# Gated linear attention and a rational MLP on one core: k's turn in the second attention bank, with a new table of steps

## The chip, the cores and the metric

One core of a Trainium2 chip runs the whole program in one launch. The metric is device time in microseconds (us). The kernel before takes 522.44 us (median of 3 runs, 521.91 to 522.75).

## The reference

Four inputs q, k, v, alpha of shape (4 batches, 8 heads, 768 tokens, 48) in float32 give a linear attention with a decay per channel; its output, seen as 3072 tokens by 384, goes through an MLP whose activation is a rational function:

```python
for t in range(S):                       # attention, per batch and head
    state = alpha[t][:, None] * state + outer(k[t], v[t])
    y[t] = q[t] @ state
h = x @ w_in                             # x: (3072, 384), w_in: (384, 2048)
P = a[0] + a[1]*h + a[2]*h*h + a[3]*h*h*h
Q = 1.0 + abs(b[0])*abs(h) + abs(b[1])*h*h
out = (P / (Q + 1e-06)) @ w_out          # w_out: (2048, 384)
```

## The kernel before

**Steps and tables.** The kernel is cut into 2737 steps. Each is a small function that issues a few instructions on one engine (SP for DMAs, PE, ACT, DVE, POOL). They are added with a name, an engine, for some a second engine (`alt`), and the steps that they must follow (`after`, lines 978 to 1185). The order in which they are issued is not worked out at run time: it is read from `ORDER` (line 77), a packed list of step numbers in which the top bit chooses the second engine. Each engine's queue holds its steps in that order. A step's costs and due times in `add` are not used when the table is read.

**Attention.** The 3072 tokens are 24 groups of 128, six for each batch. For group g: `suf` and `pre` (lines 475 and 487) are scans on DVE over alpha, which read a floor value, for g of 4 and over, from column 500 of PSUM bank 5 (`floor_q`, line 361); `k` and `q` (POOL or DVE) multiply the inputs with them. On PE come four small steps: `kt` (line 549) turns k with 4 transposes; `s` (512) makes the scores; `vk` (577) multiplies turned k with v for the state; `am` (590) multiplies the masked scores and the state with v. Between them stand `ke` (553, ACT copies the turned k out of PSUM), `qc`, `se` (523, 532, copies of the scores, ACT or DVE), `sm` (543, mask, POOL), `km`, `kv` (606, 612, DVE adds up the state), `dc`, `mc` (560, ACT or POOL puts the state beside v), and after `am` the output is copied by `xh` (ACT, 626) and `xl` (DVE, 642). All of this works in two PSUM banks, `SCB` = 4 and `SCB + 1` = 5: scores in columns 0 to 255 of both, state products in columns 256 to 447 of both, turned k in columns 0 to 447 of bank 4, the output of `am` in columns 0 to 511 of bank 4.

**MLP.** 96 units u of 128 hidden columns by 512 tokens, or the like. `in` computes h on PE in bank u mod 3; `ah`, `t1`, `rcp` (ACT), `q1` (ACT or POOL), `qm` (POOL), `t2`, `t3`, `p`, `t`, `g` (DVE) give the rational function; `oh`, `ol` (PE) multiply with w_out, after `gh` (ACT) and `gl` (POOL or DVE) have cut g into two parts. Units 0 to 9 are "plain" (lines 677 and 690), the others "wide" (700 and 714), 9 matmuls in `in` and 9 in `oh` and `ol`. `in` of unit u waits for `g` of unit u - 3, whose bank it takes.

**Weights.** 16 blocks come in as 64-bit words (`w`, SP) and are joined to float32 in four steps: `abs` (ACT 285), `low` (DVE 293), `sign` (297 on ACT, 299 on DVE), `join` (DVE 313). Then `hi` and `lo` split them for the wide units.

**The end.** 36 `gu` steps on ACT (line 863) check alpha; `vd_sum` (DVE), `vd_mm` (PE), `vd_ok` (DVE) make one number of them, which all engines read at line 1192, and a branch takes a general program if alpha is out of bounds.

The wait for the copies of the last group's output is in these lines: `was` names the steps of group g - 1 that touch the two banks.

Of the kernel before, what the change touches and what calls it, by code (L numbers as in the profile page):

```python
# [19 lines left out]
AF = mybir.ActivationFunctionType  # L20
# [4 lines left out]
class Plan:  # L25
# [49 lines left out]


ORDER = [
    'c-jq?gO(*a5CGGi?sSs1ZQHhO+qS)XcV>35wr$(CZQHi--Zxa8Qx!=~R!X6YsiG-Sq*yr>Lm3rCMOS0hI5l3)SBunQ6;-WN',
    'vD6y1L`_i3l~+?#WHnVSP)pS+bzMzT6IC}{sFnq~V-HNN(yBCSePFFh7g(WsVlV8CeXws(KkSbKaRg3NGt_D|00-e&eNL}a',
    'u~l3ZN5u<FSNqiY;K4Wq=cu`Ai`uOAs||sn7{K9}UX@m5)l4;8%~J7Ixj=4}R|N+hQrp!wbx`F~dDJEa3Mo2mRKqX~!*Pe2',  # L80
    'r?#q-DznO>f-p2F1V>_-zy+--0uQUnI0Y|itq!Q2>a<F%PN@s(naZ!qtKETJfu!nEaI!#F#YAK&2F0Y<A)|0K8WK99jwwg6',
    'C@$?$wbfpAMV(PsRXi%JE~&=qvAV3zspG1$dY~?<6Dlc<!Erb~Xd-%wL`T&mOhzdvIb~BxR9#h1)lrdY0*=M0I4$Ugnt_*f',
    '6q=54C_Y`$DJi)sqME9rs+h`5S?H>siL<boN<cSNLaMK_tKzDvT7-*(Qc)sGO;ITt&Bi&n1k+G9%1Sw@wQ8&8;sRWTX(=6@',
    'S7+5VwG;=ahw72a9<mVU;e5<N8*x+6ZDmz@%0(HdiK?b<sr%}+%1wEwASI?GREP@Ga?D8Aba|>knW!igqwD&HUV(SiTa}lJ',
    'P;q*v+Nm}wAJwILRDznTfO@VvsVb_v3Q}FvAoW8%RXtU2wGu1QDjcXPQdKHRrRa%zrCzGL>V;Z^>v1hs4yi)xuo~s30#u(G',
    'P-$uyvH=^>8}&hzq3TqF?y1$d8Mg%0q{dW>now8OS#?wGRWH>?^;Lt_5Y?K>QX6VYZK)acQ~d)S)Hb}S+fxVXNxi5y4OQi+',
    '9c{$}*fDSpo6{}*UVT)3sUIE0?y5(iHf_f`)Q5K9SM^hUQwn~oFY2HAt^geTQemnEwWI)bBn_RYGX<;RYB+sXpVThwPk+@P',
    'g<zly4WNP4l?b}gPTY-qa32n$5H&0iL?JYS_Tye`McrvI9m2yngct<I(m0w&J!n1!Qz(s49%6xoC=eYYK?0RfB??4_xDXTK',
    'Kn#cmQ6Y@R(*%kS6KN7nrf`a&BY0bf2Ex?>8cKKcQ9OntX%Q`^DKwQvQ38k!@gNZlqvLo2&*MovgVQJ>B!-K42dC3QT0$3a',
    '21Tf)w4OH5MmmLO@ieATDItT(s8T>ml?;+YCfFP@lV;Ht8ckzp6K$mfbdWCLY??#MXgRH*m2{Cts=NB0zKq-G5{*)aXceud',  # L90
    'BXpFu(+)aJ$7m-Vr(HCc)=*MN0vVwYq=ht)0aC#gyo#6U3SFm6fva?lPS8oZhWGF~?xq`f6W7u@dPI+DFYTjSco%QueSC;F',
    '=oH<gbdVa-LuNQlS>P$%qCNDCUQ%wz55*uK<b?uIK;?l{fgGwR<bs?~7z#oWI74S?Kb@od`hosM&*=r-rmXOa?oc)ut;Pgi',
    '(;NCtk@*k(r6_!!?$SSs$_3R0Dh@TF0=%UMm>nJ=@H=`>_bCZKprnjk67Eqnen>G{@nh6XoC7{kbdJFlp%PSvLV*e@ImhCh',
    'Dpw#jGbiH|oRVK-35dgn<8mr~icjz(eWGXh5}#u{{!HKK3kh3}&oA&5Cg9ZkgR*iqF2-p%EobMPoQrdC4JZdypoFRl?Vt`c',
    'hw{)AigP+H!KJt~=jM{^*mERK$cZ>TXW)!nQB?{wg9fSvROcG}gc5Tm&dgc(E#~38T!zbXKF-hOxIDkX0$d7eaZN4*wYd%#',
    '<U-tnTXJE3haa${Dix@}^`Iix<yKsYD|2ahkM;N$c7%uek!}OEp%yfT)?A+(a64|O%0e4%%Z&m(xfl25KKvVta8dq<pRfuy',
    '<i6aGt8z8&4DGoCH{!<p8NcEe{DD8QhN`J*1)6Y2?$2GI6A$2TIFLJY7w*c{pe0m?y3iVWK`ZDBO}QBda|lo7DLjJ1IGhLZ',
    'U=HP}{0INyG#<j=@gI8K5F&UakK*RsjhFCJ?#|PBC=cVAJcE^ftVi=0t`B2*E05y_&<J{PfVc57Ue2?4Hm~57+yRC{A84U^',
    'Lre8UgGRlb+e2Fz3{7AN4Cf$T#ls*RR`VJj&;LhBv);j0&*8Z|kB{+jKEZ2w9UDELPw{SU6_~*5c_Lru8$5|4U?B8|LC_OA',
    '!33BHBViQufUz*p4}hH`A_Y4gS?}UKyqBZuC|Yzhy^t620zS!$`6hRRuFxI!@qRwQFZik6z#I9Qj;?R>Ek46%c{rTr1o|!q',  # L100
    '!9705lVKBY=7StVpXUpFk?-(*P8fWMUvf+xTgTFgbmHJGe3;|txH_JWuP^as{>i^Mi9W(d`4ztz@s=NOKL|hwJmg3Gn&0tz',
    '{=@$`omM6oM!<9ZLSNy>{DiOaHI8XwnWy}h!F=G4jOG)6=2T{|*M>}N^M&J@q&k^?#{K+Um=AMc63l~8V6y_o!z`EzaZG%Z',
    '+I;1-CXF#h%m6>gCou6$LNf-!AcY<cUuhitr0=v5(uJls8B9i#$^7QzI;BppGwR$Xl}@dna~@;OH~!8)*qKBouSsk&n<OTU',
    'PHM`SEGB<wKI2VU6Uk&Xb<GqgXbPERro2h3Gw4h@x|s%1O=OeYlrxn~WmCXZ2+gCjnf|`8DPpEWQB%y+Gbv0;lf&dR*-b7}',
    '(KIks%u8L>v@^v`ebe4_Ff-tl&aAWOYNom=Y5JSlupAb_W>^NBU<)jP1rYGNU_I=FrLYhd!(Lbgjm>e$rW=NqFda=7GZV7v',
    'CZ?3BVLF-8rk3ey^65sVsmZQ8n{KA2Sq;rh-rxedw9cV(>Rft&8E6KX{JOarY=)TbriE!~TAA9Wj_F}~nqH>2$*m*INHfZ`',
    'Hf_vIGt0C!eavVx)U1JFCSdl%7&F$)Hgn8MI04&W2W*AmCdiC4!KR>ot+&H&*Z_OrG@OECa1xHfDl^`Mm<gt@S#93vwNOa+',
    'Gofa<FRa&?bx>3n(fi;r%r_IwBr`X3o>^cfn-ONM*<dcgMzhc?GEd+loPlDxxSnE4>O-(DbiLVR7MmsJ2t0)#AL{SHZnMYi',
    'HRs?04Dq+&Jlusl5N5*7G;_wBHPg*hv(L;hOU-_B&K!WUx|A*#yxEk{Wr8c{TkuvNge~R@Y&Cbya<j~wH!I9abI=?zm&^fk',
    '7!I2Y=AzkVwwrglysoG#>C5Jdxe7<jJ#*hYFh|Y9&|12-eq@fB<K~2^qATln=Dpcru9|D+gZUKt**rGa;JT@!>ju};Ps~oU',  # L110
    '%bYYyKu(#{=7zatZkwCtA)JNF5Y0S;2k;1<!w2|izL>A3s;;4{>8IwId2Xufn!3Io>QTO#@8*SxAu;8Sd9Po>5A#7^hX(qm',
    '$sif!rFm_%7#Zec%SZSGH{m{fhVO6#TIyFOjs*Mn&`^i_`0@%wqL>#D4P%%uKw+(dSsLkI#!3Ql(nLqWukZ{0fS|+1y0!Ka',
    'Nis>?uy~SC-k7&0mi#e)O>_MZew)aWSz72e!BM2CZl?d4f>KBdOCnL2SdvIK$u3DH%omXmKf-%_2L?y`cAD@fM3qWXSzbeN',
    'DIr<HvdSCCAw|QANlB?9ZFMrKD$yjmB$pJDQgTWz$t|U%w3Ly?(nPvQ5B*Vp((QFRsUfK(jdYbfl2@8ZwXmjAR^CDfT~n${',
    'EomvOq`B0VI+9O1>5jUWt}ErFn{?JKq_wn>w$dZ4r*xNIQcuSE{8B*5O9dG!!=$1#kZ!t*?ipNP8cHK+C%tuV=_7#Mbyppb',
    '_A*@hN<Zl@9VAGCWt@zcs2Jg6pvCAI86)9u_yO~!kM1a)q_ZrLQGTKfkbx2+Bjg(}{)N;M6BA)lOpK{835H6TgiC~c))Qom',
    'PlFTvAQ>zh1o4aRtEb4Mu*ot~M#(~1B#R|2Cc{{m8xvr1OpQ~epPnX5Wtqgr=`urR%0}5Nn`DVBmm#uE2561_^*}u+c!jK#',
    'I5<mY%NE%xqh*X7ltXe@j)onRVS22rl1p+~w#yDVA^{y2hwIg{MuzC2da#}&b7h{am36XHcF9P;TOP|E*(>qzxSWtHa#F6z',
    'b$KFJ<(aIPVEt96#5|Y~v*9>j0MlW1OfQ8n1s24dm>=_EF3g9gBm<t7GjdkW$rt%5`{b$Ikc@a!Zb^_HqvPXqc_H6)h`ud%',
    '<hy*65&DPxl$Y{KUdw(tAa`Ygzb9jZ@5?U<)#3WLgz0hmjl7ji_)h-U+FI+wBiZr6=jDQ2lm`;eK9u;@*+24ECi}=Xiv1_)',  # L120
    'u^KA-ULy1;{YXB_C;1?w^+-KYN3|1lG#lN<un8>K%$O)Vu}yC?*w2#DPVx!ucb&v0wLkPEUEG$iS+NvWz{;2dOJfy8t1a1N',
    'Hn~k<i(pDy!;bfv?G&HMX0h39b~{^VwJ~k1@EkUk&1rMl!kF8#O>Ils(&1%n7OZJ&*;2NwEoW=n$-15`ih1l*U*1-*v27e1',
    '*XFf#!t2^JHmz-GTiNM;hM(rA>M6Q9R>Z1U9@9!$tY|CQUbeTbZ|CaydQNa_+ctcaZfD!r_O^qarYqY9wxMlg8{6r6hMuYC',
    '>5jIOO=t7j{I(btu!U_?oaH;)g0_$CXPelWKE#f&p>~#DpnvKrwu_x&r`lh-sI6+N*`~Gx_P5pTLR}n7VprSOhS>pjpdD!k',
    '*}-;*U8KukGc00<+PS_QHnYub3)|iHur;tTw!um`-_P^YY;&xSi+uxZg2ikr3=fa6-RyMR(+;ys?J_&u&a$KIY&+VHv19Ex',
    'J0m<`XWBV-g<Wpv+Ie=oo$V*sm3Ea~te5H~I>@fJ^X&?~Qm?UV?KZpJ2HOR8p*?OV+DUe@t%d9Cdb>ui4L)HP*~NB)y<wNw',
    'n|7z&VOQ&2cDLPQ_u6Ipq+R1rhcDOr>_)rEuG9PN0ejHCw43cId)A(_OZ_c-$DXn0?IF8U-?cUIg1u<h>)*OIUb27mZ9B)`',
    'vvu&kt&3aiR{P2xwr}hPy;1+Nm+h7C*Y>S_XOGyU_LzNdAJ~Vs9)7SN?IZix{<eSYF8$YDwNLC*yIF724Y3gxvR$zycER0x',
    'kKUrU>#e#iezM>`+b{O3jqIYhs4lv@X0O|S;mV=Y?wL*Ep4+4@nR{W|<6eD2@6fGrfp38wupMsGG2A!%-9~fd{@*0m31hmB',
    'D9*ahxKAf{DO^ey%Vl*xY&Q4PrgDGvKfPbac5z&47uUse*<H?vT+TV~PU-{tpgyEe=^QS%OXK3Z1TK#|tWWD>`nXQ((zzqS',  # L130
    'd0jpi$rW?OT|$@0C3Z*k8C}wqj!5q^xJ)jy%jojE0!|T7Jy+kAa%Ei^SI(7p?Og}gz%_D>T|-yURd5wu7T3{LasymtSJ*Xi',
    'O<gnB+!b=2Tvyk^E%5{0AXmh-blqGPH`onxog=!q?rx#);R3Fw>*a>Hp{}T_>RP$hZn&%Fs=JY{maE}<yFRXttLtjJAUDd5',
    'c4OT*7wkgZEH~TDbz|HdH!ot5Z{ym!c5b!n>-xF=ZjBr7Cb)@igq!3hy9I8co8soXMQ*WM;?}yUZoLb0;ck!H>z2B+F4V1a',
    '5pJ2=;5NEVZnN9srn&v@kX!EdxdRag-Bx$lZFA?`c{kn7a5LQscfnnD_uPHA-R*D}-6glut#UivE_cLTaYx-%cg#I-k0Kts',
    '<L-nz>8`o!?xB0)p1No5z5C!kx!vxRyWzm2f9_7Zo9?4~;l8?W?xlO>wErCO#eH|TBG~_MKOK4T*8g(GpK-7MhwA-p7t_b`',
    'cU)}$+r=Fj&);=_+#8q5zjdkoJNMVc@$r2EpU_A0k$oDUZe${#)@Se;eR`kCNAXd8VxPq4_IZ3>|Id|h$|v>7d>LQX=lA)1',
    'W}n4p^>uwTAKl0B1$`l3-k0;)d?jDN7xooKR`x}FQD4zl@%4NIpWQd~jeId*)fe|od{f`pH}lDT3ZK%K@Hu==pUao@rF=EN',
    '(y#K>eGOmJFZ0WNX<y4X_bq%&-^#c4wS67m#<%q~T|3|2ckms3C*Rq3@m+m4-`)4{J$)a)!mswdd~d(juk-7Dec#vr2X6hG',
    'js',
]  # L140


# [4 lines left out]
OH = (0.722, 1.3)  # L147
# [10 lines left out]
NSC = 1  # L158
# [4 lines left out]
NQ = 3  # L163
# [14 lines left out]
def tile_gla_then_rational_mlp(ctx, tc, q, k, v, alpha, w_in, w_out, ca, cb, out):  # L178
    nc = tc.nc
    B, H, S, D = q.shape  # L180
    DM = H * D
    DFF = w_in.shape[1]
    P = 128
    C = 128
# [31 lines left out]
    def bank(n, cols=BANK):  # L216
        return ps[:, n * BANK : n * BANK + cols]


    ident = const.tile([P, P], F32, name="ident")  # L220
# [33 lines left out]
    NI = FU * P  # L254
# [87 lines left out]
    NC4 = NPAIR  # L342
# [15 lines left out]
    tq, tk = ([t[:, n] for t in tqk] for n in range(2))  # L358
# [6 lines left out]
    KW = P - GAP  # L365
    st_0, st_m, st_e = ring("st", 3, [P, NC4, D])
    kts = ring("kt", NSC, [P, NC4 * KW + GAP])
# [140 lines left out]
    SCB = 4  # L508
# [39 lines left out]

    def k_turn(g):
        for a in range(NPAIR):  # L550
            nc.tensor.transpose(bank(SCB)[:, a * KW : (a + 1) * KW], tk[g % NQ][0:KW, a, :], ident[0:KW, 0:KW])

    def k_evac(g):
        nc.scalar.activation(kts[g % NSC][:, 0 : NC4 * KW], bank(SCB, NC4 * KW), AF.Copy)

    def decay(eng, g):
        t = totals_of(g)[0:KW].unsqueeze(2).to_broadcast([KW, NC4, D])
# [502 lines left out]
    for g in range(NGC):  # L1060
        near = [("cp", *x, p, cc) for b in (SCB, SCB + 1) for x in nat_users[b] for p in (None, 0, 1) for cc in range(2)]
        was = [("xh", g - 1), ("xl", g - 1), ("km", g - 1), ("kv", g - 1), ("se", g - 1, 0), ("se", g - 1, 1)]
        add(("kt", g), "PE", 0.38, k_turn, (g,), [("k", g)] + was + near, lat=0.13)
        add(("ke", g), "ACT", 0.55, k_evac, (g,), [("kt", g), ("vk", g - NSC), "set_st"])
        add(("s", g), "PE", SV[0], sc_mm, (g,), [("k", g), ("q", g), ("ke", g)] + was + near, lat=0.13)
        add(("vk", g), "PE", SV[3], kv_mm, (g,), [("ke", g), ("sv", g, 0), ("sv", g, 1)] + was, lat=0.13)
# [158 lines left out]
```

## Time and profile before

| | |
|---|---|
| median of the 3 runs | 522.44 us |
| profiled execution, its own time | 521.38 us |
| its span, first to last instruction | 519.3 us |
| busy: PE, DVE, ACT, POOL | 499.3 (96%), 473.2 (91%), 411.0 (79%), 404.8 (78%) |
| mean granted TensorE clock | 0.993 |

Mean durations of the steps on which sums below rest, in ns, from the profile's groups by line:

| engine | steps |
|---|---|
| ACT | sign (L297) 1957, abs (L285) 940, q1 (L771) 721, t1 (L765) 684, rcp (L793) 602, ah (L762) 590, se (L539) 589, ke (L554) 548, xh (L630) 492, qc (L528) 2 x 417, dc and mc (L568) 2 x 360 |
| DVE | scans (L476, L488) 1242, turn of k and q (L473) 1238, sign (L299) 1040, join (L313) 957, p and t3 738, t and g 685, se (L541) 682, t2 677, low (L293) 565, xl 551, km and kv 342 |
| POOL | qm, gl, k, q 1290, q1 772, sm 655 |

The next instruction on ACT starts about 0.09 us, and on DVE about 0.08, before the one ahead of it ends; the sums below take each step that much shorter. "PE" rows are matmuls; a busy PE is not PE at its peak, since matmuls overlap: what one costs is read from start to start. PEld rows are its weight loads.

### The profile page before, as it was taken

Reading aid. Unit: us, or ns where it says so; the run is one execution under the profiler, and the core shown is the slowest. Engines: PE = TensorE matmul, PEld = TensorE weight load, DVE = VectorE, ACT = ScalarE, POOL = GpSimd, SP = SyncE. Lnnn points to the kernel's source line nnn. Section 1 sums busy time; section 2 is a strip of 40 time slices with the busy share of each in tenths; the row PEclk is TensorE's granted clock in tenths of the full one; section 3 lists DMA queues with packets and bytes.
Section 4 is the critical chain, followed back from the end, with each engine's and each line's share of the span. In section 5 each row is a group of like instructions: output and inputs, shape, how many; then the busy total and the mean of one; then the engine's idle time right before and its main releaser. Section 6 shows DMA issues by size and latency. Waiting matters only on the chain.

```text
span 519.3 us, 13513 instructions
## 1 busy us (share of the span) xinstructions
PE 499.3 (96%) x5094; PEld 412.3 (79%) x5094; DVE 473.2 (91%) x729; ACT 411.0 (79%) x756; POOL 404.8 (78%) x419
## 2 busy tenths in 40 slices
PE   8877899999999999999999999999999999999995
PEld 7776778788887788878888788888888787789895
DVE  3997999999999999999999999999989899898793
ACT  3879999999899877868777777886878778776564
POOL 3253765989999999788989988797896779667673
PEclk9997999999999999999999999999999999999999
DMA  9989945554555545653456454344625400050001
GB/s 246 307 240 245 279 104 130 146 119 110 119 127 136 123 92 130 106 112 84 86 120 124 93 133 84 90 86 102 143 50 116 82 1 1 3 101 1 0 1 64
DMA packets 146708, 57.56 MB, mean 111 GB/s; under 512 B 133456, under 2 KB 139216, under 8 KB 146640
## 3 DMA queue, kind: packets, MB, share of 16 engines
q1 hardware_dynamic: 146496, 56.57, 46.6%
q8 instruction: 41, 0.67, 0.5%
q14 instruction: 27, 0.22, 0.1%
q10 hardware_dynamic: 144, 0.10, 0.1%
HBM read 47.98 MB, written 4.72 MB: 101 GB/s over the span
## 4 chain that ended last, share of the span: by engine, by line
PE 63%; ACT 11%; DVE 6%; POOL 6%; DMA 5%; SPq 5%; issue 4%; POOLq 0%; DVEq 0%; ACTq 0%
PE ps L707 26%; PE ps L726 22%; PE ps L600 3%; PE ps L693 3%; SPq L415 2%; PE ps L720 2%; DMA wi_words<-in_moe_w_in_dram 2%; POOL gh_gl L819 2%; ACT wo_words L297 2%; PE ps L518 2%; PE ps L582 2%; PE ps L680 2%; POOL qm L774 1%; ACT ps L793 1%; DVE t L789 1%
## 5 line engine op out<-in xcount | busy, mean ns | idle before, releaser
L707 PE MATMUL ps<-x,wi 128*128 128x512 f32 x774 | 197.7, 396 | 0.7 <-DVE t L812 0.6
L707 PEld LDWEIGHTS ps<-x,wi 128*128 128x128 f32 x774 | 142.6, 188 | 32.6 <-DVE t L812 2.6
L726 PE MATMUL ps<-gh_gl,wo 128*128 128x512 f32 x630 | 162.5, 396 | 0.1
L774 POOL TENSOR_TENSOR qm<-qm,ah 128x512 f32<-128x512 f32 x96 | 124.1, 1294 | 23.4 <-ACT qm L771 20.3
L726 PEld LDWEIGHTS ps<-gh_gl,wo 128*128 128x128 f32 x630 | 115.8, 188 | 25.6 <-POOL gh_gl L819 0.9
L819 POOL TENSOR_TENSOR gh_gl<-t,gh_gl 128x512 fp32r<-128x512 f32 x83 | 107.4, 1297 | 21.0 <-ACT gh_gl L815 12.6
L793 ACT ACTIVATE ps<-qm 128x512 f32<-128x512 f32 x96 | 57.7, 602 | 36.6 <-DVE t L789 17.7
L803 DVE SCALAR_TENSOR_TENSOR t<-t,coef,ps 128x512 f32<-128x512 f32 x96 | 70.8, 737 | 12.7 <-ACT ps L793 11.3
L765 ACT ACTIVATE t<-ps,coef 128x512 f32<-128x512 f32 x96 | 65.4, 684 | 14.2 <-POOL gh_gl L819 9.5
L789 DVE SCALAR_TENSOR_TENSOR t<-t,coef,ps 128x512 f32<-128x512 f32 x96 | 70.7, 738 | 1.5
L785 DVE TENSOR_TENSOR t<-t,ps 128x512 f32<-128x512 f32 x96 | 64.9, 677 | 6.8 <-ACT t L765 5.2
L812 DVE SCALAR_TENSOR_TENSOR t<-ps,t 128x512 f32<-128x512 f32 x96 | 65.6, 684 | 1.5
L806 DVE SCALAR_TENSOR_TENSOR ps<-qm,ps 128x512 f32<-128x512 f32 x96 | 65.8, 685 | 0.0
L762 ACT ACTIVATE ah<-ps 128x512 f32<-128x512 f32 x96 | 56.4, 590 | 9.6 <-PE ps L707 8.3
L815 ACT ACTIVATE gh_gl<-t 128x512 fp32r<-128x512 f32 x86 | 53.6, 625 | 6.6 <-DVE t L812 5.9
L769 POOL TENSOR_SCALAR qm<-ah,bab 128x512 f32<-128x512 f32 x42 | 32.4, 772 | 18.9 <-ACT ah L762 7.1
L545 POOL TENSOR_SCALAR_AFFINE_SELECT tqk<-tqk 64x512 f32<-64x512 f32 x48 | 31.4, 655 | 18.7 <-ACT tqk L539 8.2
L771 ACT ACTIVATE qm<-ah,bab 128x512 f32<-128x512 f32 x54 | 38.9, 721 | 0.5
L476 DVE TENSOR_TENSOR_SCAN tg<-ta,ps 128x528 f32<-128x528 f32 x24 | 29.7, 1241 | 8.6 <-ACT ta L458 7.3
L720 PE MATMUL ps<-wo,gh_gl 128*128 128x384 f32 x180 | 33.7, 336 | 0.0
L497 POOL TENSOR_TENSOR tqk<-tqk,tg 128x512 f32<-128x512 f32 x22 | 28.4, 1289 | 6.5 <-ACT tqk L458 6.3
L720 PEld LDWEIGHTS ps<-wo,gh_gl 128*128 128x128 f32 x180 | 31.8, 188 | 1.2
(112 smaller groups left out, 701.5 us busy)
## 6 DMA issues: line engine op xcount, KB each, us to landing
raw_a<-in_alpha_dram SPq DMA_DIRECT2D x160, 48.0 KB, 2.2
wi_words<-in_moe_w_in_dram SPq DMA_DIRECT2D x8, 768.0 KB, 6.5
wo_words<-in_moe_w_out_dram SPq DMA_DIRECT2D x8, 768.0 KB, 6.4
sv<-in_v_dram SPq DMA_DIRECT2D x48, 96.0 KB, 2.6
wr<-in_alpha_dram SPq DMA_DIRECT2D x18, 256.0 KB, 3.1
raw_qk<-in_k_dram SPq DMA_DIRECT2D x80, 48.0 KB, 2.3
raw_odd<-in_k_dram SPq DMA_DIRECT2D x80, 48.0 KB, 2.1
raw_qk<-in_q_dram SPq DMA_DIRECT2D x80, 48.0 KB, 2.3
```

The lines of the kernel that those rows point to most:

```text
L707: nc.tensor.matmul(h_of(u), w(key)[:, kt * FU + f % FU, :], x[:, kt, xp, :], start=(n == 0), stop=(n == len(todo) - 1),)
L720: nc.tensor.matmul(bank(T_BANKS[tt], DM), g[:, tt * P : (tt + 1) * P], w(("o", f // FU))[:, f % FU, :], start=(f == 0 and first_w), stop=( ...
L726: nc.tensor.matmul(bank(O_BANKS[dt]), w(("o", f // FU))[:, f % FU, dt * P : (dt + 1) * P], g, start=(f == 0 and first_w), stop=(f == NF - ...
L765: nc.scalar.activation(buf(s, "t1", u), h_of(u), AF.Identity, bias=a2, scale=a3_reg)
L774: nc.gpsimd.tensor_tensor(buf(s, "qm", u), buf(s, "qm", u), buf(s, "ah", u), op=ALU.mult)
L785: nc.vector.tensor_tensor(t, t, h_of(u), op=ALU.mult)
L789: nc.vector.scalar_tensor_tensor(t, t, a1, h_of(u), op0=ALU.add, op1=ALU.mult)
L793: nc.scalar.add_instruction(mybir.InstActivation(name=nc.get_next_instruction_name(), engine=nc.scalar.engine, func=AF.Reciprocal, ins=[nc ...
L803: nc.vector.scalar_tensor_tensor(t, t, a0, h_of(u), op0=ALU.add, op1=ALU.mult)
L806: nc.vector.scalar_tensor_tensor(h_of(u), buf(s, "qm", u), Q_ONE, h_of(u), op0=ALU.add, op1=ALU.mult)
L812: nc.vector.scalar_tensor_tensor(t, h_of(u), 2.0, t, op0=ALU.subtract, op1=ALU.mult, reverse0=True)
L819: eng.tensor_tensor(buf(s, "gl", u).rearrange("p a b -> p (a b)"), buf(s, "t1", u), gh, op=ALU.subtract)
```

## The change

k is turned into bank 5 instead of bank 4, and `kt` of group g no longer waits for `xh`, `xl` and `km` of group g - 1 (the first three names of `was`), which read bank 4:

```diff
     def k_turn(g):
         for a in range(NPAIR):
-            nc.tensor.transpose(bank(SCB)[:, a * KW : (a + 1) * KW], tk[g % NQ][0:KW, a, :], ident[0:KW, 0:KW])
+            nc.tensor.transpose(bank(SCB + 1)[:, a * KW : (a + 1) * KW], tk[g % NQ][0:KW, a, :], ident[0:KW, 0:KW])

     def k_evac(g):
-        nc.scalar.activation(kts[g % NSC][:, 0 : NC4 * KW], bank(SCB, NC4 * KW), AF.Copy)
+        nc.scalar.activation(kts[g % NSC][:, 0 : NC4 * KW], bank(SCB + 1, NC4 * KW), AF.Copy)
...
-        add(("kt", g), "PE", 0.38, k_turn, (g,), [("k", g)] + was + near, lat=0.13)
+        add(("kt", g), "PE", 0.38, k_turn, (g,), [("k", g)] + was[3:] + near, lat=0.13)
```

`ORDER` is replaced as a whole. Unpacked, the new table has the same 2737 steps:

- 75 steps change engine: `q1` 22 times from ACT to POOL and 19 times back; `gl` 5 times from POOL to DVE, 3 times back; `mc` and `dc` 9 times from POOL to ACT, 5 times back; `k` 3 times from POOL to DVE; `se` 3 times from DVE to ACT (groups 0, 2, 23), once back (group 1); `sign` of blocks i0 and i3 from DVE to ACT; three others.
- `kt(g+1)` stands right behind `am(g)` on PE for g = 6 and g = 8 to 22, and `kt(6)` right before `am(5)`: 17 places. In the old table other matmuls stand between the two for each of these g. `s` and `vk` of one group stand side by side in both tables from group 5 on.
- `vk(2)` is issued before `se(2)`; in the old table after both `se(2)`.
- The four last `gu` and `vd_sum` are issued before `gh(95)` and `g(94)`; in the old table two `gu` and `vd_sum` come after the last copies of the output.
- The first blocks are loaded in the order i1 i0 i3 i2 o0 i4 o1 o2 o4 (old: i1 i0 i3 i2 o1 o0 i4 o2 o4).

PE's order in the first part (`tn` are transposes of the first inputs; `in(u)`, `oh(u)` in halves where a second number stands):

```
old: ... tn am.0 tn kt.1 tn s.1 tn tn in.0.0 in.1.0 vk.1 tn am.1 in.0.1 in.1.1 kt.2 in.2.0 s.2 in.2.1 vk.2 am.2
     in.3.0 in.3.1 kt.3 oh.0.0 oh.0.1 s.3 vk.3 in.4.0 oh.1.0 oh.1.1 in.4.1 am.3 oh.2.0 in.5.0 in.5.1 oh.2.1 kt.4 in.6.0
new: ... tn tn am.0 kt.1 tn tn s.1 tn vk.1 tn am.1 in.0.0 in.0.1 in.1.0 kt.2 s.2 vk.2 in.1.1 kt.3 in.2.0 in.2.1 am.2
     oh.0.0 in.3.0 oh.0.1 in.3.1 s.3 vk.3 oh.1.0 oh.1.1 in.4.0 am.3 in.4.1 in.5.0 in.5.1 oh.2.0 oh.2.1 kt.4 in.6.0
```

## Rows read from the trace of the kernel before

**Rows 1.** Stretches: length; busy PE, PEld, DVE, ACT, POOL; clock; DMA share, GB/s.

```profile
26.00:39.00 13.00, 10.22 (x192) 9.18 (x191) 12.99 (x22) 9.70 (x21) 7.39 (x8) 1.00 0.90 240
39.00:52.00 13.00, 9.62 (x124) 8.22 (x124) 9.84 (x16) 11.94 (x15) 4.68 (x7) 0.74 0.92 245
52.00:65.00 13.00, 11.54 (x169) 9.38 (x169) 12.68 (x19) 12.81 (x20) 9.76 (x15) 1.00 0.98 278
65.00:78.00 13.00, 12.00 (x116) 10.01 (x115) 13.00 (x23) 12.60 (x19) 8.83 (x10) 1.00 0.48 102
208.00:234.00 26.00, 26.00 (x251) 20.93 (x252) 25.37 (x40) 19.66 (x40) 21.66 (x21) 1.00 0.56 108
```

**Rows 2.** Waits: who waited for whom; us in total, times, longest us.

```profile
DVE t L803 <- ACT ps L793: 11.3, 21, 1.7
PE ps L582 <- ACT tqk L539: 3.4, 1, 3.4
PE ps L878 <- DVE tot_beyond L875: 2.0, 1, 2.0
DVE tg L476 <- ACT tqk L539: 1.3, 2, 1.0
```

**Rows 3.** Timeline of DVE and ACT, 38 to 45; start, us, what, idle before.

```profile
38.93 0.67 DVE L541 COPY tqk<-ps 64x512 f32<-64x512 f32 x1
40.01 0.59 ACT L539 ACTIVATE tqk<-ps 64x512 f32<-64x512 f32 x1 [3.00 <-DVE tqk L541]
40.63 0.60 ACT L793 ACTIVATE ps<-qm 128x512 f32<-128x512 f32 x1
...
44.42 0.66 DVE L812 SCALAR_TENSOR_TENSOR t<-ps,t 128x512 f32<-128x512 f32 x1
```

**Rows 4.** Timeline: ACT's first copy, rcp(3), g(3), and in(6) on PE.

```profile
8.19 1.08 ACT L458 ACTIVATE ta<-ps 128x512 f32<-128x512 f32 x2 [5.81 <-PE ps L439]
...
61.17 0.77 ACT L793 ACTIVATE ps<-qm 128x512 f32<-128x512 f32 x1
...
65.75 0.67 DVE L812 SCALAR_TENSOR_TENSOR t<-ps,t 128x512 f32<-128x512 f32 x1
...
67.26 2.77 PE L680 MATMUL ps<-x_whole,wi_words 128*128 128x256 f32 x12
```

**Rows 5.** Timeline of PE, 180 to 193: kt(10), am(10) and wide matmuls.

```profile
180.20 0.55 PE L551 MATMUL ps<-ident,tqk 112*128 112x112 f32 x4
180.52 1.63 PE L726 MATMUL ps<-gh_gl,wo 128*128 128x512 f32 x6
...
186.69 2.20 PE L707 MATMUL ps<-x,wi 128*128 128x512 f32 x9
188.73 0.84 PE L726 MATMUL ps<-gh_gl,wo 128*128 128x512 f32 x3
...
190.54 2.33 PE L726 MATMUL ps<-gh_gl,wo 128*128 128x512 f32 x9
192.71 1.31 PE L707 MATMUL ps<-x,wi 128*128 128x512 f32 x5
```

**Rows 6.** Timeline of PE behind am(0): eight transposes, then kt(1).

```profile
18.23 1.09 PE L439 MATMUL ps<-ident,raw_second 128*128 128x128 f32 x8
19.16 0.55 PE L551 MATMUL ps<-ident,tqk 112*128 112x112 f32 x4
19.54 0.28 PE L439 MATMUL ps<-ident,raw_second 128*128 128x128 f32 x1
```

**Rows 7.** Timeline, 193 to 195: a scan on DVE and kt(11) on PE.

```profile
193.31 1.25 DVE L476 TENSOR_TENSOR_SCAN tg<-ta,ps 128x528 f32<-128x528 f32 x1
...
193.85 0.55 PE L551 MATMUL ps<-ident,tqk 112*128 112x112 f32 x4
```

**Rows 8.** Timeline of the end: SP issues the last stores, and the verdict.

```profile
512.56 2.09 SPq L759 DMA_DIRECT2D out_dram<-parts  x4
...
515.80 0.15 DVE L881 TENSOR_SCALAR ok<-ps 1x1 int32<-1x1 f32 x1 [0.28 <-PE ps L878]
```

More of the change, by code (lines that the diff above doesn't have):

````diff
@@ L77 @@
 ORDER = [
[L78 to L137, printed above, removed]
@@ L138 @@
-    '(y#K>eGOmJFZ0WNX<y4X_bq%&-^#c4wS67m#<%q~T|3|2ckms3C*Rq3@m+m4-`)4{J$)a)!mswdd~d(juk-7Dec#vr2X6hG',
-    'js',
+    'c-jrtgMuBp768!fWFtv!+qP}nwr#hkGt*IR+qP}nwr$_O_Z4eRQA%m$)l?Nr#ZgYhP|*~rm<m-C6<v)};}xq3YJrNXrm2N$',
+    'm0GPPs>y1STBKH}H7d4Rtd^*yYMJVxmj`<4UOKHxr`D<sf$3_c>a7Rr^s0~UuLtP9x}RRB)~k(bupXrc=^1LK+M;%-ohq)1',
+    'ulB2W>W0b?7^2Ua^X5WuMwLJ%R73SJJy*?BTUDr@rRJ#NI-qB(?dp&!tIDeis$5`~+N3tC5gOFUpdcNl!}V#ES6x&|)m61m',
+    'JymtpS+!SPR>46bIzms;ht+&lQEgNC)$V{%2UVoLXf7Fz29vAH!FvMv)B$xYa73jD6i@{fB8LbbRfHB};%GfakJaP!G(A0N',
@@ new lines @@
+    'hIUwAB~vNYcs*55(37;sSQs1Q;4D2`C&#QRyUL+bU`kAd6ZK@BP0iF-OcacdQ858V!|0e5V_-HsrOv36>WaFi(&9}OHzXb=',
+    '#6*}56XPwF1XG7tbzEIF_0%;pN2kG}>V&$ao~XIHxXP)LVlr%?8mgwMxhjm$)j9P_rN<1I1Lx_*dZAvVmjun%+3~i@jZ1Y4',
+    'RZNvo8F7JL7PLZNH#bbqkX)Dti(oM<ifvUUtcd5;1@%&0S0z<5l^5Ho_Nuq)t8NCD#7C;Cs;=_ka$O25VP(vWS+Itxrt)J|',
+    'e4rkx$LftLfW<@ZsFnJiDuJc33|7JFSQhW9O}ZM^R4r8p)lt>Q2G|fc2Q>~^rTeJWdaYikH|UMJ39i@uR6#6+jj)S)t)8j(',
+    '>V<l%%3%$>rvmD}TBEn<|I`Q77RzG=?4|~(A!=*TcHIs?sgJ5A*21o8n{JA=affb(b+9gWSN+vcHCPQ(JyeitkGITi(*ZkT',
@@ new lines @@
+    'Cv1)_@Sr}gJE_iro~l=1ryigN26|&3?2GlVAO29^)K~RaeOCX}F5MYh;up1BcfqdM3R`0UzpHov@LMVPss5;6DkfOyh67Pl',
+    'u<DNkusaSy10&TQy;twk`*jbD4KW}pc+h}wSdYXuI1b0-U<|@w48agZFa$$!D2CxMoPbC4Aw670gD8+l#ez8CpeOdii8ux0',
+    '!z5%lppWU}T3{4T#c+(kQR=9^WA2(rObC;48cxU2I3E{aVzm$#<8T~-i*PBP&?ogNeO8~=BLbm;B^ah6RHRB0n1RV5E<}d}',
+    'und=DxJm+N^f{dfX5s}s3uog+y#Y7kCLDufaWfvoL%0Gj>BNu}R^m3?f?M&fPNh;oN=OE&Aq8Yom-Q8$7Scdr$Ov<AF0R5$',
+    'cp0~27D%n`nfvCdzOJw7(dsa+#x)_CRhGaG+=)l<I9|b{cns47cHw<}6>s1P+>JN%ZGA`I#FKamALyI<mcFO2g*?=!F&mu0',
@@ new lines @@
+    'dAJtW;d<PIkMRjU!$<mod1x{~X2=ieAU$M)tWW@6;9h)=ukbqF!rM4ToyC`!6JFyT%no;PAMVHBcmUtvTYQIq@Gt(uJdhXi',
+    'K}pD^azi0i7ivOns0x*#0#t%RPzS0&33!j^@ISnVK<DwXzJO6F8bzm=^Z_qoVO1KE(b&KPe2B?OQw~sM2<bjP!cX`S-{=?=',
+    'o1W;mIt8VqTo8*sW03$+9EwX!LY7idZk3wSP&|63pXx98T))zJ0<U#iice)AJLRBUl#UWm2`WiBDIq1I7dkiPp`Z8_zoVn4',
+    '=qU;%rX-Y<(o;RiKzS)6)udXKk1DCks!E_B6oqO~3reZtPz;Jd4X6$+p*g(MAM|fsit<wdDoAChES08ml!-D^7RpM6s1?1}',
+    'g{d}`rwY^nTGLCNjf&7mT?)#<C*4T3f{M@rDpDP)Pk(e>Dy_-{IzcT}l!{R$s!YA94|Ran&=%T2ae8FhQX8s5WuXCeplVc|',
@@ new lines @@
+    'KI_NktFA{4sS!1%zSNHD!vGip&7dkZR{g0Tm4`37Jv9k5p{CS~22c%ZPA#Y-b)tsQ4mv|0XbQm;LM`c={;q%OAG)^srRxMb',
+    '(?IG%gJ>}Q)m>={O{Gy3N?{aE-KaYap`kR4hSO47Mm?w}MNngC53STN=no@k8vUnd&`jzIku;i?QzIBd|Fk#LX%?-Zv9yv_',
+    'kutLhOfL%1NE%1mXghU-C+4Zq2F)C50>+G|)~Zcl0<EUGG>_)f8d^&Wh)fVIr0&oUI>J!s0zF_I^@R~&4I44e?4;v#f+o@=',
+    'noNsmF-0*uXxFISw4S1xXyzoHqUa`(*+3g<6ODvDbe2w2PdGz2=qBx@AlOGsXfwqyx9ORQX|~W->IH*g5DbTb5P<!3fNs&9',
+    'QFrONiDhD&-Vn!}qw{o-UeYVNM;GWK-KRrzgpN{NbC`}%0+Y}r4$ffWnfT@sU8dLch91x_3Ww1U36o*4kANu<3`tB<^N=3V',
@@ new lines @@
+    'V|q^?C<NZpZ~9CB=nDNuz{$)D^U`R3M^ES}eWXv6++3w=be*2jbBfJz_%ls|FQj-B7)B<J%ke`Ka6C@PDa=>;MxihU2Kb3E',
+    '7Q)~cPJ+3x99~cwPRrlv52fQ&CZ%B(ww#xL&`(OliFrDVhY2tarb0%O*(Bi%p&5CoPtTb+lSysTn0zLG@JvW&l5%Et>^UE2',
+    ';bfeg%W)Jg&oiI^=jVc)-lX7)oYoBV6*wzr<Lq3Y8}K6dhAUtm6y_ovm1FW^_<_;65HEoRFdvq}9+(5OVIgdX9k2|tm<^EC',
+    'RN)+4iBobaPR+SEH?M@ET#PqCajwcGxC3|OZ0402<Qwv9Q<<xAb)E$|xe@2#)lh?*a!Jl%vYSp^lLzu3F3n}QacC)S#+|tv',
+    'H{s^of?IM<(<QVk*W$rko4a!lZp8&mPwvINc@5+;tvQb=XohfEj^H|6m+Ns`j^v@C!?+D^h25|U3Yp=&1vbMj*b6&hBV2;B',
@@ new lines @@
+    'unpEhZZnH#b31O&qqz@{;kB?H%9^~UusI6HU<3zvh#$*yxGxtm```pzgfnmo#`8!H;$ZH_t9cDi;5X*2nac~fs3~rWnQ=Uk',
+    '7xE;Y%u_goNAX(j&jWZJ&*S+#l}niYZ~)4iMZB1oa7h!&dw4HT<NaL99ELCs=jl9y55iL3$Y*&OpX2qR<$^cxK0d$|%po|$',
+    'n|L!<G&6YxujJ*tiqG=}E^Q8S8B@s|fjZ_moP^7;g}3rWzQl+52w&!He3Xyz72eJ}xUvcOr|<}Zd=>M~9OtV%(x2dyd>&52',
+    '1$Ykk;JvvD*Z4Z$;Cp<ZAMm5l$NZ4r^9TOObxl=M%~Us^_$EK$r~Hg}@-E)ZHB3!Y%hWcvSP94}KFw$NHV^aX;6B`fD{uoo',
+    '^B4Zg&-n#wK_R&Y^~`Wz-@N2+Ji_1MyBtem%PW4vci|yCgFA2=8kiSw9d5!aFv9YkfACKh`NeUiq4{7w8Y@n`G%}6NZ;m3b',
@@ new lines @@
+    'xwVNW3FS4s<#*h~G&AwTnwqwzy-6f*AgYA=a372RzytUVU*IErhbQn09>Zt&318t8#NcQg?7u-KNg$c!FBg^~@`tlZV#y-S',
+    '&3~Lkl1ehkAvq<QWD9F)ib+u^F3II3MAg|Pm$WngIJ(4;I8sHbN;QcoDJ7Mpkkpb}N=hE7A*JLm<dvq<!jzD=!1_J>0I!{n',
+    'siW!AQbx*3IjJuBB)^3DX3|Z%OPk<Urh};^X{5Gfkd7vu6p(^aNXkn^X(7!e#J853(o*V3U8yJaWw?xx3ewBGgC5e!^fnFT',
+    'lj$jyq_Q-U#?nUqL9eh@(pDNuA899_%?IdWI-A}Skde|?+DnLZkWs#$bd;{9n;9ia2ZaSosC1I?GC?NEMCmUBWU@>Vt7GUf',
+    'KCQ&k{{d>zVG=F_Wso$H&N5iKo2e2ZkupuDOCJ+kcag3#S{BGc*(jT2u`H4$VLePw6XC~t(ivrljPqM$vqbu#GEBzESV^v<',
@@ new lines @@
+    '>$EzGo*^@3nSh=pvt_Gj-8Z<ONvz}Q<+5FN$WmD$D<z&zs?+HdI+32_lj&`;Q+CN0Guo%u<9&ZKz#Nisa#)VYTv;Vw&1%^#',
+    'dt{ERk)vYtKr_e$%n3Oumt~$@ktZ@=p2}b|%&e33GQu1Si=&UrDLE}`<(ll3DgLTFlaXe)*(c8>$RyBXO%i=Z&dQMB4ElwP',
+    '3%)Kl<g0v>4YFSj$U(U&@%1fvC9fru9%_QkZMh?p{W<wAcjcwLk+<^AgqTt0f?SmIa!G#31V7Q=llziTe>b5f+=Q9YhOOA&',
+    '@<)D#{gS_8?E`UkjCm(M{JngThw?}g*n~Eb&977H)Vi?Ft8?pAI;T#fGwMP*ht8u5>g@VI`6tSbHxo@%8_mw}xpZ|MVWQaR',
+    'wx%ws3+Re^s-Iv!N@Dw1KFMeKB9Ug2`C+o^7&fMjWn<f9Ho2W_rWmk4O_K0ACaFzfwJokw+Eg~P&Z1M>j5d?aVzY&3w<WEy',
@@ new lines @@
+    'XiHhLacw+X%f_+sZB|>_=CHMGPMa;Lj4f-+>-17V7tv|#bf3#kHPcKwo8Fet<!w1z!B(`hd|I2q=C*lkSzT4<)5UZZ-BOp+',
+    'b!{D6FMOVvADq{=w$sfFlg}2g1??=;z*e#iZGGFwwy|w(Wn0BowfSv3J2$wHZETy^lDe=hV$0~tx`l3P7nnYFrkQO@>ArTM',
+    'X`~mK_I8@@Xgk@WHnW}Sf0+<F$`-fPZ3kP;*042gGuy(pw9V~m)7kd31H!x5TDq(4W~bU|cCjg~!)$-s-G<sh_O}^q2ihTa',
+    'iCJn|*`7As_OR1!6J1GH(>3&LA8AM12s_3OwZrUiJJyb~GwgU<N7vP}?HoJ82JD*PWoD+GWtZ9IcBNfm*Vwgom0fP;+Ie<@',
+    'U1{dqUbeR#X}8<ecAcGQSD77lm)&W1+dVeO2HQz?fn8`%*v5LEU*PBZMYfG@u8Y~Gy0vboOW4|az1?6p+P!v@-DgkQ)3$!l',
@@ new lines @@
+    'IXl@-v77B;yTsnKOYIiB-=4B_{CvN}H`52~LA%zhH|xwHd&|DEukB%b+upG&%$e}BcB|cBcA0v5qd9MngkP{1?Iqh@Z?i}3',
+    'G5f~;F?Yl7*-hrH{cE<E270r(Zy(r)_OiWV--W-oTg^7J-Rv+Q>?8ZwezZ^QC;QoU)SdKkd(Hl~f9!P|)m^o_%~Si#{%4o@',
+    'zxH3aay!iz`_=9-o%J_+!#=ms+zb2CCUZY*a<|v)H{i50F1kzM+Ui!io$jE~eGgCRVz@3r`^*7z(2!#n+r@D)BVxIqHoN=v',
+    'e_H-C-E>^{&n)!a^<k67rFHRKeAiVUGDpl&bKF>$Dk8N@=T4eqCV@-nobxV<%i&76k}jvq<xZP3CcVqx^16&JpF3er1)nvg',
+    'T_RV;m3N6<5|`8|1Z?2Sx=b#M%N>!&<#!ca0awtKa}`}?*U&X`ja?I0$YpieTqRf8RdH2aVb{zxb<JH1SH!h+tz2u@(RFfN',
@@ new lines @@
+    'TxZwa^>Bk+H8<D|b#2@bH^Oy|=;nI5Uaq$*>WaDIuDa{vhDAiW8m^`bxLU4`tLN&w(QdYz<J!96Zmb*QM!E@Zq6>1tuAOV|',
+    '`nnFTzZ>8}+#0vm^>YK=TsO{*caz*?H{UIAqg<E^ccomYi*QriRJYg7a|_)fH_gp(Gu?Ez)UWdE+=hsaZn0bMHo47ii(BHB',
+    'x>;_STkcl4MSh<<;P$(N5r^DXx6Pe%=iNnj!Ci9O-41uz9d=jT5x3H<a`)W>x7zJ;yWLK=$6a+t-7$CEop2xANB7WObJyJs',
+    'x7a_9c;ZgFNA9UR?M}I8?zvm*Ke;dNv-|39I`C)QEqB|Ub$8qg_tL#`uiYD`eQbZ%-E(pLH}~EBaI5`K_sbbik?4QBKmRX=',
+    '_3WMZKCX`+nZUnw@7#Nr#;5i1d=#J1NA-z(VxPoE^Z&WLKA%tLGx)y|>3ve4%>Q%ce14zFXZF#3a$mrg_sVDVS$x6BLcXxC',
@@ L140 @@
+    '>z4Z!zKAdCv-)g4yN}^x`dGe#PvI;2N|D8UabLn$@l|~epVP1O^?d{1$XE7_eKTLpSNAo1bKfMgsZZ%s`P4p_&+YU0HNK=T',
+    '<y-i5zNW9`Yx~l^j4$i!_`1HOZ{=J2Hok3SJ>Sl^_qAOI-_dvSoqZSI)pzsVeGlK$_wv1cKi|-=_kDa{-`{WW{{!wOoel',
 ]
````

## The prediction, made before the change was run

> **What bounds the kernel now.** I read the busy time by stretch first, then the waits, then the timeline at the places that they name. From about 80 us to the end of the wide units PE has no gap: it is busy 26.00 of 26 us between 208 and 234, with DVE at 25.37 and ACT at 19.66 [rows 1]. So the program takes PE's own time, plus what PE loses before it is filled, plus the end. What PE loses before is large: it is busy 10.22, 9.62, 11.54 and 12.00 of 13 us in the stretches from 26 to 78, and from 39 to 52 its clock is 0.74 on average, between the levels 2.4 and 1.2 GHz [rows 1]. From 52 to 78 DVE (12.68 and 13.00) and ACT (12.81 and 12.60) are as good as full, so a lead there has to be earned by less work or by idle time taken out earlier: ACT is idle 3.30 us between 26 and 39, DVE 3.16 between 39 and 52 [rows 1].
>
> The reader is to see one event in this. PE's longest wait of all is 3.4 us at `vk(2)` (L582), for a copy of the scores on ACT (L539) [rows 2]. That copy itself sat 3.00 us behind the other half of the same copy, which the old table gives to DVE (L541, start 38.93) at the end of a row of other DVE steps [rows 3]. `vk(2)` writes other columns than the copies read, but in the same two banks.
>
> **The change part by part.** All sums go against the profiled execution's 521.38 us (span 519.3 and 2.1 around it), which is 1.06 under the median of 522.44; I add the 1.06 at the end.
>
> *The front, ACT.* In the old table the steps between ACT's first copy and `rcp(0)` sum to 24.2 us (durations of the table above, each less its 0.09 of overlap); they start at 8.19 [rows 4] and `rcp(0)` starts at 40.63 [rows 3], so ACT idles 8.2. In the new table they sum to 27.3: two `sign` at 1.87, two halves of `se`, one `dc` and one `abs` come in; one half of `se`, `ah(1)`, `t1(1)`, `q1(0)` and an `abs` go out. I walk the new order with the same durations. `se(0)` and `se(2)` are now on ACT in one piece and `vk(2)` is issued before `se(2)`, so the 3.00 us are gone; I find waits of 0.7 (first copies) and 0.5 (for `am(1)`). `rcp(0)` then starts at 8.19 + 27.3 + 1.2 = 36.7, 3.9 us earlier. From `rcp(0)` to `rcp(3)` both tables hold 20.8 us of ACT work; the old one took 61.17 - 40.63 = 20.54 [rows 3, 4], so it went without idling, and the lead holds at 3.9. To `rcp(12)` the new table has 0.3 more: 3.6.
>
> *The front, DVE.* Up to `g(0)` the new table has 3.2 us less DVE work, up to `g(3)` 2.2 less (two `sign`, two `se` halves and one `q` fewer, `k(3)`, `xl(3)` and one `se` half more, and another order). Old starts are 44.42 and 65.75 [rows 3, 4]; the walk gives about 40.1 and 61.0, leads of 4.3 and 4.7. Up to `g(12)` 1.6 come back, of which 0.7 is a real addition (`gl(11)`): a lead of 3.1 to 4.0.
>
> *The front, PE.* The same set of steps stands before `in(6)` in both tables. With `g(0)` at 40.7 and `g(3)` at 61.5 (ends) the walk starts `in(6)` at 61.6 against 67.26 [rows 4], 5.7 earlier. PE can't keep more of it than ACT and DVE feed: the lead that lasts is ACT's 3.6. A walk sees no wait that nobody planned. DVE waited for `rcp` 21 times, 0.54 us each on average [rows 2]; I keep back two of them, 1.1. **Front: -2.5**, ends 0 and -5.7.
>
> *The turn behind the values.* The rate of the wide matmuls is (188.73 - 186.69) / 9 = 0.227 us. Nine behind `am(10)` take 192.71 - 190.54 = 2.17, so leaving an attention visit of this kind for wide matmuls costs 2.17 - 2.04 = 0.13 [rows 5]. `kt(10)` alone costs 180.52 - 180.20 = 0.32 and no entry worth naming [rows 5]. Side by side, the 0.13 behind `am` falls away, but the turn then pays for coming out of `am`: the eight transposes behind `am(0)` take 0.93, where the four of `kt(1)` take 0.095 each for 112 columns, which is 0.109 for 128 and 0.87 for eight: 0.06 more [rows 6]. That leaves 0.07 for each of 17 places, 1.2. Ends: +0.06 each if nothing falls away and the entry is paid (+1.0), and -0.13 each if the entry is hidden (-2.2). **-1.2.**
>
> The Trainium skill, TensorEngine Tiling (Array Packing), section Key Properties, says that changing the tiling mode drains TensorE. By it the number of drains stays as it was, since `kt` and the wide matmuls both use the full array and only `am` doesn't; the sum would then have 0 here in place of -1.2. The 0.13 behind `am` and none before `kt` [rows 5] agree with the rule on where a drain is paid; what a turn pays behind `am` is measured at one place only [rows 6].
>
> *The wait taken off `kt`.* `kt` follows `am` without waiting for the copies of `am`'s output. In the steady part PE had other matmuls to fill that wait, so this alone is worth 0.
>
> *Bank 5.* New is that `kt` writes, and `ke` reads, the bank in which DVE's scans read the floor. In the old trace scans run across `kt`: the scan at 193.31 lasts until 194.56 and `kt(11)` starts inside it, at 193.85 [rows 7]; I find 5 such turns among groups 4 to 23, and not one scan across `s` or `vk` of these groups, which write bank 5. Scans wait for copies of the scores instead, 1.3 us in two waits [rows 2], though they share no column with them. So from now on a turn that meets a scan waits it out. In the new table a scan stands right before `kt` in two places (groups 18 and 22) and one PE step before it in five (7, 10, 14, 16, 19). PE loses between 0 and 7 x 1.24 = 8.7. I take one wait of the size seen, 1.3 / 2 = 0.65: **+0.6.**
>
> *The end.* The verdict's sum waits 2.0 us for the last two checks [rows 2] and `ok` is written at 515.95 [rows 8]. In the new table checks and sum are done before the last matmuls, and `ok` would come at about 514.1. All engines then read it, SP only when it has issued its last store at 514.65 [rows 8]; it read at 515.98. That is 1.3, less 0.1 because the last store has to land: **-1.2**, ends 0 and -1.3. The checks stand earlier on ACT, which has time to spare there.
>
> Other engine changes in the steady part move work off POOL to ACT, which is at 19.66 of 26 [rows 1]: 0. Sum: 521.38 - 2.5 - 1.2 + 0.6 - 1.2 = 517.1, and with the 1.06 between the profiled execution and the median **518.2 us**.
>
> **The rivals.**
> 1. *The lead is lost again.* ACT has 3.1 us more to do up to `rcp(0)`, and between 52 and 78 it had no room [rows 1]. If new waits eat the lead, the other terms stay: 522.44 - 1.2 + 0.6 - 1.2 = 520.6. For it: ACT and DVE both full. Against: the taken-out idle time is plain to see.
> 2. *The lead is lost and the turn gains nothing*: 522.44 + 0.6 - 1.2 = 521.8. The drain rule named above would bring the second half of it.
> 3. *Bank 5 holds PE* (the other side). One mechanism: `kt` stands in PE's queue right behind `am`, and everything behind it waits while a scan in bank 5 ends. Price up to 1.24 for each of the seven places, 8.7 in all; it decides from 4.9 us on, four of the seven in full, and at its worst gives 518.2 - 0.6 + 8.7 = 526.3. For it: the pattern of rows 7 and the missing overlaps of `s` and `vk`. Against: those two had the same neighbours, and PE never waited long for a scan. The Trainium skill, PSUM — Partial Sum Buffer, section Terms, says that no two of the three engines may access the same bank within the same partition at once, reads against reads included; the trace agrees as far as no scan crosses `s` or `vk`.
> 4. *A new gap halves the clock.* After the 3.4 us wait the clock fell to 1.2 GHz, which is what the 0.74 says: 0.52 of 13 us, 6.8 us, at half [rows 1, 2]. If a new gap of that kind comes up (before `am(1)` the walk has one of 2.4), the loss is up to half of 6.8, 3.4: 518.2 + 3.4 = 521.6.
>
> **How the numbers follow.** What a measurement of this kernel can tell from no change is about 0.2%, 1.0 us. The forecast has 0.55, its own range 516.0 to 520.5; rival 1 0.16, rival 2 0.11, rival 3 0.12, rival 4 0.06. Faster: the forecast, most of rival 1 (0.13), and a part of 2 and 4 (0.05), 0.73. The same: 0.03, 0.07, 0.02 and 0.02 of the rivals in order, 0.14. Slower: 0.13, nearly all of it rival 3. The range goes down to 514.8, where most of the front's 5.7 is kept, and up to 522.8, which takes in rivals 1, 2, 4 and the mild part of 3; below it I leave 0.06 and above it 0.12.
>
> **What would show it.** In the trace after: `in(6)` should start at 61 to 64 us and `rcp(3)` at 57 to 59; the wait of L582 for L539 should be gone and PE's clock in 39 to 52 be back near 1.00. L551 should follow L600 directly in 17 places, the four transposes taking some 0.38 there, with no entry of 0.13 in front of the next wide matmul beyond what `kt` shows now. No scan should cross L551 any more; waits of PE's L551 for DVE's L476 or L488 would be rival 3, and their sum its price. The verdict should be written about 0.6 us after the last matmul. The prediction is wrong in its main step if `in(6)` starts no earlier than 66, and wrong in its sign if PE waits more than 4.9 us in all at L551.

## The result and the profile after

The kernel after takes 515.4 us (median of 4 runs, 515.21 to 515.66) beside 522.6 of the kernel before (521.91 to 523.51): ratio 0.9869, 95% interval 0.9849 to 0.9888. Beside a later group of runs it took 514.42 against 521.80, ratio 0.9857 (0.9838 to 0.9876). The forecast was 518.2, with a range of its own of 516.0 to 520.5 and a whole range, rivals included, of 514.8 to 522.8.

Line numbers of the kernel after are those of before less one (`kt` L550, `vk` L581, `am` L599, scans L475 and L487, `ke` L553, `se` L538, `rcp` L792, `g` L811).

The stretches after, with the columns of [rows 1]:

```profile
26.00:39.00 13.00, 10.61 (x218) 9.36 (x218) 11.93 (x20) 11.98 (x22) 4.37 (x8) 1.00 0.87 202
39.00:52.00 13.00, 11.73 (x186) 10.21 (x186) 12.51 (x20) 12.83 (x20) 7.92 (x10) 1.00 0.85 242
52.00:65.00 13.00, 12.55 (x116) 9.93 (x114) 12.83 (x22) 12.89 (x17) 7.86 (x12) 1.00 0.94 240
208.00:234.00 26.00, 26.00 (x294) 21.14 (x293) 25.31 (x41) 21.59 (x43) 22.17 (x24) 1.00 0.52 102
```

The clock from 39 to 52 is back at 1.00. ACT is idle 1.02 us from 26 to 39, where it was 3.30, and DVE 0.49 from 39 to 52, where it was 3.16. The waits after, with the columns of [rows 2]:

```profile
PE ps L517 <- ACT kt L553: 2.6, 2, 1.3
PE ps L550 <- DVE ps L382: 1.3, 1, 1.3
PE ps L550 <- ACT tqk L538: 1.0, 1, 1.0
```

The waits for `vk(2)` and for the verdict are gone. New are `s(2)` and `s(4)`, which wait for ACT's copies of the turned k (L553), 1.3 us each, and two of the turn: `kt(1)` waits for DVE's write of the floor column (L382), `kt(3)` for ACT's copies of the scores (L538). Only the wait of `kt(1)` is owed to bank 5: the copies of the scores read both banks, and `kt` follows them in both kernels. Now the marks of [rows 3, 4]: `rcp(0)` and `rcp(3)` on ACT, `g(0)` and `g(3)` on DVE, `in(6)` on PE:

```profile
40.43 0.60 ACT L792 ACTIVATE ps<-qm 128x512 f32<-128x512 f32 x1
...
61.20 0.58 ACT L792 ACTIVATE ps<-qm 128x512 f32<-128x512 f32 x1
...
44.13 0.68 DVE L811 SCALAR_TENSOR_TENSOR t<-ps,t 128x512 f32<-128x512 f32 x1
...
64.92 0.65 DVE L811 SCALAR_TENSOR_TENSOR t<-ps,t 128x512 f32<-128x512 f32 x1
...
65.63 2.86 PE L679 MATMUL ps<-x_whole,wi_words 128*128 128x256 f32 x12 [0.58 <-DVE t L811]
```

They come 0.2 earlier than before, no earlier, 0.3, 0.8 and 1.6. The end: the last pieces on PE, the verdict's sum and `ok`:

```profile
506.01 2.37 PE L734 MATMUL ps<-wo,gh_gl 128*128 128x384 f32 x12
508.31 0.19 PE L877 MATMUL ps<-ones,tot_beyond 128*1 128x1 f32 x2
...
509.06 0.14 DVE L880 TENSOR_SCALAR ok<-ps 1x1 int32<-1x1 f32 x1
```

`ok` starts 0.7 us behind the last pieces (508.38). From these to the end of the span (513.1) it is 4.7 us; before, 513.53 to 519.3, 5.8.

And a turn beside the values, `am(10)` and `kt(11)` on PE, to set beside [rows 5]:

```profile
190.82 1.10 PE L599 MATMUL ps<-tqk,sv 128*32 128x64 f32 x64
191.85 0.60 PE L550 MATMUL ps<-ident,tqk 112*128 112x112 f32 x4
192.22 1.62 PE L725 MATMUL ps<-gh_gl,wo 128*128 128x512 f32 x6
```

The four transposes take 0.37 us (forecast 0.38), 0.05 more than the 0.32 of `kt(10)` alone in [rows 5]. `kt` stands so in all 17 places.

So the 6.15 us between the profiled executions (521.38 and 515.23) divide into three parts. `in(12)` starts at 105.13 in place of 106.40, which is 1.3. From there to the end of the last pieces it takes 403.25 in place of 407.13, which is 3.9. The end gives 1.05. The forecast had 2.5, 0.6 and 1.2.

### The profile page after: what moved, and what is told of

Same layout as the page of the kernel before. It is cut to its first block, busy times and chain, and to the rows that moved or that the text cites. A ratio compares the mean times of both kernels' runs of the same rounds, so it can differ in the third digit from the quotient of the medians.

```text
span 513.1 us, 13534 instructions
## 1 busy us (share of the span) xinstructions
PE 497.0 (97%) x5094; PEld 413.6 (81%) x5094; DVE 472.6 (92%) x731; ACT 417.9 (81%) x765; POOL 397.0 (77%) x408
## 4 chain that ended last, share of the span: by engine, by line
PE 62%; POOL 3%; SPq 3%; DVE 2%; DMA 1%; issue 0%; ACT 0%; POOLq 0%; ACTq 0%
PE ps L706 27%; PE ps L725 22%; PE ps L719 6%; PE ps L599 3%; SPq L414 2%; PE ps L517 2%; PE ps L581 1%; PE ps L550 1%; POOL gh_gl L818 1%; POOL qm L773 1%; DMA out_dram<-parts 1%; POOL tqk L496 1%; PE ps L734 0%; DVE t L802 0%; POOL tqk L544 0%
## 5 line engine op out<-in xcount | busy, mean ns | idle before, releaser
L706 PE MATMUL ps<-x,wi 128*128 128x512 f32 x774 | 192.9, 393 | 0.1
L725 PE MATMUL ps<-gh_gl,wo 128*128 128x512 f32 x630 | 159.7, 394 | 0.0
L818 POOL TENSOR_TENSOR gh_gl<-t,gh_gl 128x512 fp32r<-128x512 f32 x81 | 104.8, 1297 | 22.3 <-ACT gh_gl L814 14.5
L792 ACT ACTIVATE ps<-qm 128x512 f32<-128x512 f32 x96 | 57.8, 602 | 29.6 <-POOL qm L773 15.2
L811 DVE SCALAR_TENSOR_TENSOR t<-ps,t 128x512 f32<-128x512 f32 x96 | 65.7, 684 | 1.4
L768 POOL TENSOR_SCALAR qm<-ah,bab 128x512 f32<-128x512 f32 x45 | 34.8, 772 | 23.9 <-DVE wi_words L312 6.7
L475 DVE TENSOR_TENSOR_SCAN tg<-ta,ps 128x528 f32<-128x528 f32 x24 | 29.9, 1244 | 8.8 <-ACT ta L457 8.8
L770 ACT ACTIVATE qm<-ah,bab 128x512 f32<-128x512 f32 x51 | 36.7, 722 | 0.6
L496 POOL TENSOR_TENSOR tqk<-tqk,tg 128x512 f32<-128x512 f32 x19 | 24.5, 1288 | 8.8 <-DVE tg L475 7.0
```

Source lines behind the costliest of these rows:

```text
L706: nc.tensor.matmul(h_of(u), w(key)[:, kt * FU + f % FU, :], x[:, kt, xp, :], start=(n == 0), stop=(n == len(todo) - 1),)
L725: nc.tensor.matmul(bank(O_BANKS[dt]), w(("o", f // FU))[:, f % FU, dt * P : (dt + 1) * P], g, start=(f == 0 and first_w), stop=(f == NF - ...
L792: nc.scalar.add_instruction(mybir.InstActivation(name=nc.get_next_instruction_name(), engine=nc.scalar.engine, func=AF.Reciprocal, ins=[nc ...
L811: nc.vector.scalar_tensor_tensor(t, h_of(u), 2.0, t, op0=ALU.subtract, op1=ALU.mult, reverse0=True)
L818: eng.tensor_tensor(buf(s, "gl", u).rearrange("p a b -> p (a b)"), buf(s, "t1", u), gh, op=ALU.subtract)
```

## The experiments

All ran beside the kernel before, which took 521.8, 521.8 and 521.2 us in the three groups. Ratios are to it, with 95% intervals.

**First group: the bank, the turns, the floor, the front.**

Bank alone (`e1`): the old table, with the diff of the bank and of `was`.

> The kernel before (522.6 us) with one thing changed: k is turned in bank 5, and kt no longer waits for xh, xl and km; the table of steps is the old one. Theory (the bank by itself gives nothing, the new table gives all): no gain, and the five turns of groups 4 to 23 that a scan crossed in the trace before now wait for its end, 0.1 to 1.2 us each: 522.6 to 525, I take 523.5. Rival A (the wait taken off kt is itself worth something): 521 or less. Rival B (bank 5 holds PE in full at each of the five): 522.6 + 5 x 1.24 = 528.8.

537.20 us, 1.0301 (1.0287 to 1.0315): 15.4 slower, worse than rival B. PE waits for scans only 2.8 us at L551. The larger part goes the other way, DVE waiting for the turn. The timeline of its DVE, from 62 to 70:

```profile
62.73 0.72 DVE L803 SCALAR_TENSOR_TENSOR t<-t,coef,ps 128x512 f32<-128x512 f32 x1
67.48 1.25 DVE L476 TENSOR_TENSOR_SCAN tg<-ta,ps 128x528 f32<-128x528 f32 x1 [4.02 <-PE ps L551]
...
69.92 0.66 DVE L812 SCALAR_TENSOR_TENSOR t<-ps,t 128x512 f32<-128x512 f32 x1
```

and of its PE, from 66 to 71:

```profile
66.89 0.55 PE L551 MATMUL ps<-ident,tqk 112*128 112x112 f32 x4
70.63 4.54 PE L680 MATMUL ps<-x_whole,wi_words 128*128 128x256 f32 x12 [3.19 <-DVE t L812]
```

The scan stands behind `kt(4)` in the table, and `kt(4)` comes at 66.89 because PE has other work ahead of it. DVE stands still for 4.02 us with everything queued behind the scan; then `g` is late and PE waits 3.19 for it. Scans also wait for `ke`, which only reads the bank, as they do; the waits of DVE's scans, 12.2 us in these three lines:

```profile
DVE tg L476 <- PE ps L551: 5.0, 2, 4.0
DVE tg L476 <- ACT kt L554: 4.2, 4, 2.1
DVE fp L488 <- PE ps L551: 3.0, 1, 3.0
```

Turns apart (`e2`): the kernel after, each of the 17 turns one wide step further back, as here:

```diff
-... am.11 kt.12 oh.28.0 oh.28.1 ...
+... am.11 oh.28.0 kt.12 oh.28.1 ...
```

> The kernel after (515.4 us) with the 17 turns that stand beside a group's values moved one step of wide matmuls further back (ke behind its kt where needed); bank 5, engines and all other steps stay. Theory: only the entries come back. In the two traces a visit of am and kt with its exit costs 0.063 us less than the two apart, so 17 x 0.063 = 1.07 and 516.5 us. Rival A (standing side by side gains nothing): 515.4. Rival B (the turns side by side are where most of the 4 to 5 us between 110 us and the end comes from): 519 or more.

534.02 us, 1.0242 (1.0228 to 1.0256). The number is rival B's, but its reason isn't: in some places the table had a scan between the two positions, and `kt` now waits for it. The timeline of its PE at `kt(6)`:

```profile
101.39 1.01 PE L550 MATMUL ps<-ident,tqk 112*128 112x112 f32 x4 [3.34 <-DVE tg L475]
```

Three such waits sum to 10.5 us, and the clock falls with them (0.86 on average from 91 to 104). The experiment measured a wrong order, not the turns; `e7` below does it again.

Floor late (`e3`): the kernel after with one DVE step moved.

```diff
-... sign.i1(ACT) am.0 ... kt.1 ... (fl ahead of all of these)
+... se.1.1 fl kv.1 ... (fl behind the second copy of the scores of group 1)
```

> The kernel after (515.4 us) with DVE's write of the floor column in bank 5 (L382) moved from ahead of the second turn of k to behind the second copy of the scores of group 1, still ahead of the first scan that reads it. Theory (the front's lead was lost to bank 5): the 1.30 us wait of kt(1) goes, and with it the 3.41 us at half clock right behind it, 1.7 us of PE's time. At most 3.0 us: 512.4; since ACT and DVE have to follow, I take half of it, 513.9. Rival (the front is paced by ACT and DVE, PE's wait is only where it shows): 515.4, the wait turns up at another line.

513.40 us, 0.9838 (0.9825 to 0.9852), the lowest median of all. It is 1.0 under the kernel after (514.42 in `c_after` below), but the two intervals overlap, so the gain isn't clear of the noise. The profiled executions differ in the clock. Stretches of the kernel after, columns as above:

```profile
20.00:22.00 2.00, 1.72 (x9) 1.64 (x10) 2.00 (x5) 1.99 (x2) 0.00 (x0) 0.61 0.89 279
22.00:24.00 2.00, 2.00 (x12) 1.79 (x11) 1.98 (x4) 1.80 (x5) 0.07 (x1) 0.54 1.02 251
```

and of the one with the late floor:

```profile
20.00:22.00 2.00, 0.71 (x13) 0.37 (x15) 1.93 (x4) 2.00 (x3) 0.00 (x0) 1.00 0.75 196
22.00:24.00 2.00, 2.00 (x70) 1.73 (x67) 2.00 (x3) 1.93 (x6) 1.01 (x1) 1.00 1.13 338
```

In the one PE had waited 0.99 and 1.30 us shortly before, and the clock, 2.4 GHz up to then, was at 1.2 for most of the four microseconds. In the other it stayed at 2.4, though the wait itself only moved: `s(1)` now waits 1.29 us for `ke(1)`.

That the wait at `kt(1)` alone brings the clock down is not shown. `e2` has the order of the kernel after up to `kt(6)`, and in it `am(0)` and `kt(1)` wait the same 0.99 and 1.31 us, yet its clock held:

```profile
20.00:22.00 2.00, 2.00 (x23) 1.74 (x25) 2.00 (x4) 2.00 (x3) 0.00 (x0) 1.00 0.82 261
22.00:24.00 2.00, 2.00 (x70) 1.73 (x70) 2.00 (x3) 1.93 (x6) 0.98 (x1) 1.00 1.00 261
```

From `am(0)` on PE to `rcp(0)` on ACT it is 22.56 us in the kernel after, 21.15 in `e2` and 21.20 in `e3`. So in these traces 1.4 us go with the half clock, and none that shows with the wait. Run by run the clock decides less: three of the five runs of `e3` have a mean clock of 0.996, as the kernel after has, and they took 512.75 to 513.75; where it fell in them no trace shows.

New front in bank 5, old rest in bank 5 (`e4`):

> The new table up to the values of group 6 (about 113 us in the trace after), then all steps that are left in the order and on the engines of the old table; k in bank 5 throughout. The parts that follow have no turn beside the values. Theory: the front brings what PE shows there, 1.3 us, and the old rest keeps its stalls and its five crossings of scans: 521 to 523.5, I take 521.8. Rival (the front is worth more than PE shows there, because ACT and DVE come out of it with a lead that pays later): 519 or less.

529.38 us, 1.0136 (1.0120 to 1.0151): a miss. `in(12)` starts at 105.31, as in the kernel after, so the front is there; but the old rest then loses 10 us, with waits of the kind seen in `e1`. It can't tell what the front is worth; `e8` can.

**Second group: the same questions, with the order against the scans kept.** The kernel after, unchanged (`c_after`):

> The kernel after, unchanged, beside the others of this group, so that a microsecond can be told: 515.4 us, or 514.6 if it moves with the kernel before, which took 0.8 less with the first group of experiments than when the two were compared first.

514.42 us (513.20 to 515.25), 0.9857 (0.9838 to 0.9876).

One wide step between `am` and `kt` (`e7`): here the wide step is drawn ahead, and `kt` keeps its place in the table, in 15 of the 17 places (groups 7, 9 to 16, 18 to 23).

> The kernel after (515.4 us) with one step of wide matmuls put between am and kt in 15 of the 17 places, by drawing that wide step ahead, so that each kt keeps its place in the table against DVE's scans (moving kt itself past them is what cost 18.6 us in the experiment before). Theory: only the entries and exits come back, 15 x 0.063 = 0.95, so 516.3 us, and no wait of L550 for a scan. Rival A (side by side gains nothing): 515.4. Rival B (kt right behind am is what keeps it out of the scans' way): 518 or more, with DVE's scans waiting for L550.

516.85 us, 0.9907 (0.9892 to 0.9922), 2.4 over `c_after`. The two traces are the same to 0.03 us up to `in(12)`, at 104.69 in both. Then `am(10)` and `am(23)` start so in PE's timeline of `c_after`:

```profile
190.33 0.88 PE L599 MATMUL ps<-tqk,sv 128*32 128x64 f32 x48
...
431.70 1.10 PE L599 MATMUL ps<-tqk,sv 128*32 128x64 f32 x64
```

and in the one with the step between:

```profile
190.91 0.30 PE L599 MATMUL ps<-tqk,sv 128*32 128x64 f32 x6
...
433.81 0.31 PE L599 MATMUL ps<-tqk,sv 128*32 128x64 f32 x6
```

That is 0.58 and 2.11 later. From one `am` to the next it grows by 0.07 to 0.11 in 11 places (mean 0.094), by 0.30 to 0.42 in three, where other steps came to wait as well, and by nothing in one. The forecast had 0.07 a place.

New front, old rest with k in bank 4 (`e8`), and old front with k in bank 4, new rest (`e9`), both cut behind `am(6)`:

> The new table with k in bank 5 up to the values of group 6 (some 113 us), then the rest of the old table with k in bank 4 as before, so that no turn of the old rest meets a scan's bank. Theory (the front is worth what PE shows there): 521.8 - 1.3 = 520.5 us. Rival A (ACT and DVE come out of it with a lead that pays later): 518 or less. Rival B (all of the gain lies in the rest): 521.8.

> The old table with k in bank 4 up to the values of group 6, then the rest of the new one with k in bank 5 and the turns beside the values. Theory: it brings what the two traces show from in(12) on, 3.9 us, and the end, 1.05: 521.8 - 4.95 = 516.9 us. Rival (the rest lives on the lead of the new front): 519.5 or more.

520.03 us, 0.9955 (0.9939 to 0.9971), and 518.30 us, 0.9933 (0.9921 to 0.9946). The front brings 1.8 (1.5 to 3.2 by the interval), the rest with the end 3.5 (2.8 to 4.1). About 2 of the 7.4 of the whole change are in neither. In `e9` 1.4 of these are lost at the cut: `in(12)` starts 1.8 later than in `c_after`, `in(20)` 3.2 later. In `e8` the profiled execution, its slowest, takes 1.0 more from `in(12)` to the last pieces than the kernel before (408.09 against 407.13).

**Third group: the reasons given for the front and the end, and where the floor lies.** `vk(2)` first (`e10`), in the kernel before:

```diff
-... s.2 se.2.0 se.2.1 ... in.2.1 ... vk.2 km.2 ... am.2
+... s.2 vk.2 se.2.0 se.2.1 ... in.2.1 ... km.2 ... am.2
```

> The kernel before (521.8 us beside these runs) with one step moved: vk(2) ahead of the two copies of the scores of group 2 and of in(2,1), so that PE's longest wait, 3.4 us of L582 for L539, and the 6.8 us at half clock that go with it can't arise. If PE kept all of it: 3.4 + 3.4 = 6.8, 515.0 us. Theory (PE can't run ahead of ACT and DVE, which are full from 52 to 78 us, so what stays is about what the whole new front brought, 1.3 to 1.8): 520.3 us. Rival A (nothing stays): 521.8. Rival B (most of it stays, the new front spoilt it in another place): 518 or less.

521.37 us, 1.0003 (0.9994 to 1.0012): nothing, rival A. The timeline of its PE:

```profile
36.20 0.67 PE L582 MATMUL ps<-sv,kt 64*64 64x48 f32 x30 [0.74 <-DMA sv<-in_v_dram]
36.80 1.60 PE L680 MATMUL ps<-x_whole,wi_words 128*128 128x128 f32 x12
43.62 1.94 PE L600 MATMUL ps<-tqk,sv 128*32 128x64 f32 x64 [5.22 <-DVE st L610]
```

`vk(2)` runs 5.5 us earlier, and PE waits 5.2 at `am(2)`, for a sum of the state that DVE reaches at 43.13 in its own order, 42.99 before. `am(2)` starts at 43.62, before at 43.48, and the clock falls to half as it did, for 6.8 us. DVE is held by ACT there: `p(0)`, three steps ahead of that sum, waits 1.67 us for `rcp(0)`. And ACT still sits behind DVE's half of the copy, as in [rows 3], so that `rcp(0)` starts at 40.77:

```profile
40.15 0.59 ACT L539 ACTIVATE tqk<-ps 64x512 f32<-64x512 f32 x1 [3.46 <-DVE tqk L541]
```

So the experiment took away PE's wait, but not the split of the copy between two engines. `se(2)` whole on ACT in the old table, the other half of what the new one does there, was not run.

Floor in bank 4 (`e11`), on top of `e1`:

```diff
-    floor_q = ps[:, 5 * BANK + 500 : 5 * BANK + 501]
+    floor_q = ps[:, 4 * BANK + 500 : 4 * BANK + 501]
```

> The kernel with the old table and k in bank 5, which took 537.2 us, with one thing changed: the floor column that the scans read moves from bank 5 to column 500 of bank 4, where k was before. Theory (the 15.4 us are turns, their copies and scans that wait for each other because floor and k share a bank): most of it is gone, 522 to 526 us, I take 524, since the scans now share a bank with the values' output instead. Rival (the 15.4 us come from k in the bank of the scores, or from something else): 533 or more.

549.17 us, 1.0532 (1.0517 to 1.0546): the theory as put falls. The waits for the turn are gone, but in bank 4 the scans meet `am` and the copies of its output, and that costs more. PE's waits, with the columns of [rows 2]:

```profile
PE ps L600 <- DVE fp L488: 4.9, 2, 2.8
PE ps L600 <- DVE tg L476: 2.9, 1, 2.9
```

DVE's waits:

```profile
DVE tg L476 <- PE ps L600: 5.5, 2, 3.5
DVE fp L488 <- ACT x L630: 5.2, 2, 4.4
DVE tg L476 <- ACT x L630: 4.3, 2, 3.2
```

What it shows is that the price hangs on the table's order against whoever shares the scans' bank, not on bank 5 as such.

Checks last (`e12`), in the kernel after:

```diff
-... oh.92 ol.92 gu.17.1 ... vd_sum g.94 ... gh.95 ... wd.5.3.192 last vd_mm wd.5.3 ...
+... oh.92 ol.92 ... g.94 ... gh.95 ... wd.5.3.192 gu.16.1 gu.17.1 last wd.5.3 ... vd_sum vd_mm
```

> The kernel after (514.4 us beside the last group of runs) with the last two checks on ACT, their sum and the verdict put back behind the last pieces of output, as in the old table. Theory: the end gets longer by what the two traces show between the last wide work and the end of the span, 5.77 - 4.72 = 1.05 us: 515.5. Rival (the end is set by the last store, the checks are hidden): 514.4.

516.00 us, 0.9887 (0.9870 to 0.9904), 1.6 over `c_after`, though the two intervals just overlap. The trace is clearer. Its last pieces end at 508.77, the span at 514.5: 5.7 us, as in the kernel before. The verdict's sum waits again, as PE's timeline has it:

```profile
510.81 0.19 PE L877 MATMUL ps<-ones,tot_beyond 128*1 128x1 f32 x2 [2.05 <-DVE tot_beyond L874]
```

Floor late and `kt(3)` behind `in(2,0)` (`e13`):

> The kernel with the late floor write (513.4 us) and one more step moved: kt(3) behind in(2,0), so that it no longer waits 1.0 us for ACT's copies of the scores in bank 5 (L538). Theory (ACT and DVE pace the front, and PE only waits in another place): 513.4. Rival (PE's waits are what the front is long by): 512.4.

514.01 us, 0.9852 (0.9839 to 0.9866): no gain over `e3`; the two intervals overlap. From `am(0)` to `in(12)` it takes 85.78 us, `e3` 85.86. `kt(3)` no longer waits; PE does at another line, in its waits up to 110 us:

```profile
PE ps L692 <- DVE t L811: 1.3, 1, 1.3
```

## Why the prediction was right, and where not

The time lies in the whole range, 2.8 us below the forecast's value and 0.6 below its own range. That the number came so near is in part luck: the front was put 1.2 us too high and the steady part 3.3 too low, each for a reason that the prediction did not see. The range went down to 514.8 for a front that keeps most of its 5.7, and that is not what came.

**The front (-2.5; the trace shows -1.3, `e8` -1.8).** This step failed: the path that it took through ACT, and with it the size. The walk let ACT start at 8.19, gave it 27.3 us of work and 1.2 of idle time, and so had `rcp(0)` at 36.7. The stretch from ACT's first copy to `rcp(0)`, with the columns of [rows 1], in the kernel before, the kernel after, `e2` and `e3`:

```profile
8.19:40.63 32.44, 25.10 (x452) 22.56 (x450) 30.28 (x46) 24.34 (x49) 12.20 (x14) 1.00 1.00 283
9.18:40.43 31.25, 24.35 (x452) 21.05 (x449) 27.65 (x43) 27.62 (x50) 10.99 (x13) 0.95 0.95 250
8.26:38.10 29.84, 23.93 (x452) 20.98 (x449) 27.69 (x43) 27.41 (x50) 10.95 (x13) 0.96 0.96 259
8.23:38.13 29.90, 22.79 (x452) 19.81 (x449) 27.63 (x43) 27.50 (x51) 10.97 (x13) 1.00 0.96 258
```

ACT's work came as walked, 27.6, and the 3.00 us behind DVE are gone. But ACT was idle for 3.6 us, not 1.2, and began 1.0 later. So its lead of 3.9 at `rcp(0)` came out as 0.2, and at `rcp(3)`, forecast for 57 to 59, as nothing. Of the idle time 1.2 belongs to the half clock of 20 to 24: PE's transposes of the inputs were late, and ACT's copies of them. `e2`, which has the wait of `kt(1)` but not that half clock (its 0.96 comes from 35.6 to 39.0), has 2.4, as `e3` has without either. The late start is not the table's alone: `e2` and `e3` have the same first steps, and ACT began at 8.26 and 8.23. The walk had neither the floor write nor the clock in it.

The one event, `vk(2)`'s wait, was also misread in part. `e10` takes PE's wait away, and the time stays: behind it stood `am(2)`'s wait for DVE, which ends at the same moment, and behind that ACT's copy. What the split copy costs by itself is open. That ACT and DVE pace the front, rival 1's reason, is what `e10` and `e13` point to: in each a wait of PE is taken away, and no time is gained. PE nevertheless kept 1.3 to 1.8, with DVE's `g(3)` 0.8 earlier; which of the front's moves gave it wasn't separated.

**The turn behind the values (-1.2).** Right in mechanism and near in size: 0.094 in place of 0.07, so 1.6 for 17 places, and up to 2.4 with what else `e7` set off. The forecast's 0.13 saved and 0.06 paid come from [rows 5, 6]; the trace after has 0.05 paid at `kt(11)`. The rule of the Trainium skill that was weighed there (TensorEngine Tiling (Array Packing), Key Properties), that a change of tiling mode drains TensorE, would have given 0 if only the number of drains counted. The 2.4 us of `e7`, whose interval lies above that of `c_after`, show that this count alone doesn't give the price.

**Bank 5 (+0.6).** In the steady part the new table pays nothing: the lists of waits name no wait of L550 for a scan behind 110 us and no scan that waits for L550. The bank cost in the front instead, 1.3 us of PE's waiting at `kt(1)`, where the forecast had looked at groups 4 and up only. And the bound of 8.7 was too low as a price: it counted PE waiting for scans and left out the other direction, DVE waiting for the turn with `g` behind it, which is the larger part in `e1`. Rival 3's mechanism is real; the new table keeps clear of it. In `e1` scans also wait 4.2 us for `ke`, a read for a read. The Trainium skill (PSUM — Partial Sum Buffer, Terms) counts reads against reads among the accesses that two engines may not make to one bank at once. The trace agrees in that the scans wait; what the chip does where nothing makes them wait, no run here shows.

**The end (-1.2).** Right: 1.05 in the trace, and 1.0 in that of `e12`, whose median is 1.6 over `c_after`.

**What the forecast did not have.** From `in(12)` to the last pieces 3.9 us went, against 0.6 forecast. Counted from one matmul's start to the next over both traces, the parts are roughly these: attention visits and the gaps behind them 1.5 (the turns), waits of over 0.13 us 0.9 (1.23 in four, after 0.34 in two), the last pieces 0.5, and 0.9 in small delays of single matmuls. Where a visit is held to end moves some tenths between them. The step that hid this was to read PE as without a gap from its 26.00 of 26 us busy [rows 1]. A busy share of one stretch shows no wait elsewhere (from 390 to 416 us the same view has 25.61 of 26) and no gap that the matmul before it covers. `e9` shows that most of this gain belongs to the new rest of the table and not to the new front; which of its moves on POOL, ACT and DVE took the waits away stays open.

**Rivals.** 1 holds for ACT's lead but not for the sum. 2 and 3 didn't come. 4 came in small: behind the new gap at `kt(1)` the clock was at half for 3.4 us, in six of the seven profiled executions that have this gap and in none of the two without it (`e3`, `e13`).

## What to carry to other kernels

A wait in the list is worth what stands behind it: before pricing it, take it away in the order, ask which wait of the same engine then ends last, as that of `am(2)` did, and follow that one back through the other queues, here to ACT's copy. Where two engines' steps share a PSUM bank, a written-out order binds both ways; look for the scan that waits behind a late matmul as much as for the matmul that waits for the scan, and move neither past the other unseen (18.6 to 19.6 us here). A merge of two PE visits is worth measuring with the order against all other engines kept.

## What the runs showed that was not expected

The same bank move costs 15.4 us with one table and is part of a gain of 7.4 with another. The wait of 1.3 us at `kt(1)` didn't show up to `rcp(0)` by its length; what showed, 1.4, was the half clock behind it, and one execution (`e2`) had the wait without the half clock. Standing beside `am` a turn saves 0.09 us, though the number of changes between full and divided array is the same.
